# Experts 2 to 5: their weight loads moved behind the last group but one of the eighth tile

## The chip, the cores and the metric

The kernel runs on one core of one Trainium2 chip. The time is device microseconds of one execution. Before the change three runs took 494.34, 494.59 and 498.18 us, median 494.59. One more execution was profiled: it took 492.98 us, of which the profile covers a span of 491.1 us. All times of single instructions below are counted in that span, from its start.

## What is computed

The program filters a signal along its sequence in the frequency domain, and then sends the 19,968 resulting rows through a mixture of eight experts in which every expert keeps at most 80 rows:

```
X = rfft(x, axis=1);  y = irfft(X * (filt_r + i*filt_i));  x = y.reshape(19968, 256)
probs = softmax(x @ w_gate);  expert_idx = argmax;  gate_w = probs of that expert
for e in range(8):
    tok = rows of expert e, of these the 80 with the largest gate_w
    out[tok] = gate_w[tok] * (relu(x[tok] @ w1[e]) @ w2[e])      # all other rows stay zero
```

x has shape (8, 2496, 256), w1 (8, 256, 1024), w2 (8, 1024, 256), all in fp32. One expert's two matrices are 2 x 1024 KB.

## The kernel before

**Stages.** Up to about 300 us the kernel transforms the eight batches and multiplies their spectra with the filter; the spectra go to memory in `yf`, and the gate's logits give the 80 rows that each expert keeps. At most 128 rows a batch are kept, so from there the kernel works on eight tiles of 128 rows, one a batch. For tile t, `fetch` gathers rows of the inverse transform's table (tiles `gts`, two tiles of rows in a buffer), `spectrum` loads the batch's spectrum (`yb`), `turn_rows` transposes the rows on TensorE (L487) with a ScalarE copy (L491), and `add_rows` multiplies them with the spectrum (L498). Each tile goes in five groups of four, and the list `work` holds the groups' transposes ("t") and products ("m") in the order in which TensorE gets them; `go(n)` emits the next n. At the end of a tile the result is copied to `yr` (L503, for the last tile L505 and L506) and written to `y_sel` in memory from ScalarE's queue (L508).

**The experts.** `Experts.gather` (L1040) fetches an expert's 80 rows from `y_sel` by an indirect DMA of GpSimd. The gathers of experts 0 to 2 are emitted before the eighth tile is finished and read only what tiles 0 to 6 wrote; rows of the eighth tile are added by `turn` from `yr` on the core (L1058, beside L1056). So these three gathers wait for the write of the seventh tile's rows. `turn` transposes the rows (L1053 or L1056) and copies them to `xs` (L1061), `layer1` (L1070) and `layer2` (L1085) are the two matrix products, and the result is scattered to `out` (L1090). The order on TensorE is turn 0, layer1 0, turn 1, layer1 1, turn 2, and then for each e: layer2 e, layer1 e+2, turn e+3.

**Order.** The whole is in a manual schedule: each engine gets its instructions in the order in which the code emits them, and waits only for semaphores. Place in the code therefore does not tie a load on SyncE's queue (SP) to a place on TensorE; it ties it to its neighbours on the same queue, and to whatever used its buffer last.

**Weights.** `load_weights` issues two DMAs of 1024 KB on SP (L217 for w1, L219 for w2). Experts 0 and 1 have buffers of their own, asked for after tile 4. Expert 2's buffer is one of the two of `t1pool`, asked for after tile 5, and in the built program it is the one that held the table rows of tiles 4 and 5. Experts 3, 4 and 5 are emitted inside the expert stage, behind `turn(0)`: expert 3 in the spectrum buffer `yx`, expert 4 in one of `ypool`, expert 5 in the other buffer of `t1pool`, which held the rows of tiles 6 and 7. Experts 6 and 7 take the buffers of 0 and 1 when these are done. SP's queue thus holds, in this order, w0, w1, w2, w3, w4, w5, w6, w7.

```
for e in range(NO):
    ex.gather(e, 128 * (B - 1))
go(len(work))
ex.extra = st["yr"], st["last"]
for e in range(3):
    ex.turn(e)
    if e == 0:
        weights(3, st["yx"], "ys")
        weights(4, ypool, "ys")
        weights(5, t1pool, "t1")
```

Of the kernel before, what the change touches and what calls it, by code (L numbers as in the profile page):

```python
# [13 lines left out]
F32 = mybir.dt.float32  # L14
# [9 lines left out]
B, S, C = 8, 2496, 256  # L24
# [13 lines left out]
NDB, NFC = C // 128, FF // 128  # L38
# [43 lines left out]
def kernel(  # L82
# [100 lines left out]
    ypool = ctx.enter_context(tc.tile_pool(name="spec", bufs=NY))  # L183
# [31 lines left out]
    def load_weights(e, w):  # L215
        w1s[e] = w[:, 0:NDB * FF].rearrange("p (k f) -> p k f", k=NDB)
        nc.sync.dma_start(out=w1s[e], in_=moe_w1[e].rearrange("(k p) f -> p k f", p=128))  # L217
        w2s[e] = w[:, NDB * FF:NDB * FF + NFC * C].rearrange("p (k d) -> p k d", k=NFC)
        nc.sync.dma_start(out=w2s[e], in_=moe_w2[e].rearrange("(k p) d -> p k d", p=128))  # L219

    def gather_gates():
        nc.gpsimd.memset(gate[:], 0.0)
        for e in range(E):
            nc.gpsimd.indirect_dma_start(
                out=gate[:, e:e + 1], out_offset=None, in_=gates_dram[:, :],
                in_offset=bass.IndirectOffsetOnAxis(ap=idxt[:, e:e + 1], axis=0),
                bounds_check=N - 1, oob_is_err=False)
# [5 lines left out]
    with ExitStack() as actx:  # L233
        bctx = ExitStack()

        def pool(name, bufs, space=None, within=actx):
            kw = {} if space is None else {"space": space}
            return within.enter_context(tc.tile_pool(name=name, bufs=bufs, **kw))
# [3 lines left out]
        t1pool = pool("t1", 2)  # L242
# [19 lines left out]
        st = {}  # L262
# [204 lines left out]
        def fetch(t):  # L467
            if t % 2 == 0:
                gts[t // 2] = t1pool.tile([128, 2, NS * 128], F32, name=f"gts_{t}", tag="t1")
            nc.gpsimd.indirect_dma_start(  # L470
                out=gts[t // 2][:, t % 2, :], out_offset=None, in_=rows[:, :],
                in_offset=bass.IndirectOffsetOnAxis(ap=idxb[:, t:t + 1], axis=0),
                bounds_check=S - 1, oob_is_err=False)

        def spectrum(t):
            p = ypool if t % NE < NE - 1 else st["yx"]
            ybs[t] = p.tile([128, NS, C], F32, name=f"yb_{t}", tag="ys")
            nc.sync.dma_start(out=ybs[t], in_=yf[t])

        def weights(e, p, tag):  # L480
            load_weights(e, p.tile([128, 2 * NFC * C], F32, name=f"w_{e}", tag=tag))

        def turn_rows(t, g):
            ps = fps.tile([128, SG, 128], F32, name=f"pw_{t}_{g}", tag="f")
            for i in range(SG):
                s = SG * g + i
                nc.tensor.transpose(ps[:, i, :], gts[t // 2][:, t % 2, 128 * s:128 * s + 128],  # L487
                                    ident[:])
            if g % 2 == 0:
                wts[t, g // 2] = xpool.tile([128, 2, SG, 128], F32, name=f"wt_{t}_{g}", tag="x")  # L490
            nc.scalar.copy(out=wts[t, g // 2][:, g % 2], in_=ps[:])  # L491

        def add_rows(t, g):
            if g == 0:
                pos[t] = yps.tile([128, 2, 512], F32, name=f"po_{t}", tag="y")
            for i in range(SG):
                s = SG * g + i
                nc.tensor.matmul(pos[t][:, 0, 0:C], lhsT=wts[t, g // 2][:, g % 2, i, :],  # L498
                                 rhs=ybs[t][:, s, :], start=(s == 0), stop=(s == NS - 1))
            if g == NS // SG - 1:  # L500
                yr = t2pool.tile([128, 2, C], F32, name=f"yr_{t}", tag="t2")
                if t < B - 1:
                    nc.scalar.copy(out=yr[:, 0, :], in_=pos[t][:, 0, 0:C])  # L503
                else:
                    nc.scalar.copy(out=yr[:, 0, 0:128], in_=pos[t][:, 0, 0:128])  # L505
                    nc.vector.tensor_copy(out=yr[:, 0, 128:C], in_=pos[t][:, 0, 128:C])  # L506
                st["yr"] = yr[:, 0, :]
                nc.scalar.dma_start(out=y_sel[128 * t:128 * t + 128, :], in_=yr[:, 0, :])  # L508
# [223 lines left out]
        with tc.manual_schedule():  # L732
# [113 lines left out]
            work = []  # L846
# [8 lines left out]
            def go(n):  # L855
                for kind, t, g in work[:n]:
                    if kind == "t":
                        turn_rows(t, g)
                        if g == NS // SG - 1 and t == NE:
                            fetch(6)  # L860
                            fetch(7)
                    else:
                        add_rows(t, g)
                        if g < NS // SG - 1:
                            continue
                        if t + 3 < B:
                            spectrum(t + 3)
                        if t == NE:
                            gather_gates()
                        if t == 4:  # L870
                            weights(0, wpool, "w")
                            weights(1, wpool, "w")
                        if t == 5:
                            weights(2, t1pool, "t1")
                del work[:n]

            go(1)
            logits(B - 1, 0)
            go(1)
            logits(B - 1, 1)  # L880
            for part in range(4):
                gating(NP - 1, part)
            go(4)
            gating(NP - 1, 4)
            gating(NP - 1, 5)
# [37 lines left out]
                         y_sel[0:128 * B, :], out, idxg, idxs, gate, w1s, w2s)  # L923
            for e in range(NO):
                ex.gather(e, 128 * (B - 1))
            go(len(work))
            ex.extra = st["yr"], st["last"]

            for e in range(3):
                ex.turn(e)  # L930
                if e == 0:
                    weights(3, st["yx"], "ys")
                    weights(4, ypool, "ys")
                    weights(5, t1pool, "t1")
                if e < 2:
                    ex.layer1(e)
            for e in range(E):
# [556 lines left out]
```

## Time and profile before

| what | value |
|---|---|
| median of three runs | 494.59 us |
| the profiled execution's own time | 492.98 us |
| its span | 491.1 us |
| TensorE busy, of the span | 451.3 us (92%) |
| mean of all DMA traffic | 230 GB/s, 112.79 MB |
| end of the eighth tile's last product | 404.3 us |
| layer1 of expert 0 starts | 410.27 us |
| layer1 of expert 2 starts | 432.84 us |

In the timeline each line gives start, duration, engine, source line, operation, tiles out<-in, the number of instructions merged, and in brackets the idle time of that engine before it and what ended it. "SPq" is the issue of a DMA on SyncE's queue, and its duration is that of the issue, not of the transfer. In the table of windows each row is a stretch of time with, for each engine, busy time and (x) the number of instructions, then the granted TensorE clock (1.00 is full speed), the mean busy share of the 16 DMA engines and GB/s.

### The profile page before, as it was taken

What the parts mean: (1) busy time and instruction counts of PE and PEld (TensorE: products, weight loads), DVE (VectorE), ACT (ScalarE), POOL (GpSimd) and SP (SyncE); (2) the same over time, 40 slices, a digit from 0 to 9 for tenths busy, and PEclk for the clock granted to TensorE, in tenths of its full rate; (3) what the DMA queues carried; (4) which work ended last, traced back from release to release, by engine and by line L of the source; (5) the groups of instructions that cost most, each with busy time, mean ns of one, the idle gap of its engine ahead of it and who ended that gap; (6) DMA issues with size and microseconds to landing.
All of it is one profiled execution on the core that took longest, in us unless ns stands there. A gap on an engine that the chain in (4) does not pass through costs nothing. (4 is left out here: it accounts for less than half of the span.)

```text
span 491.1 us, 8653 instructions
## 1 busy us (share of the span) xinstructions
PE 451.3 (92%) x3382; PEld 423.1 (86%) x3382; DVE 202.7 (41%) x582; ACT 221.7 (45%) x339; POOL 176.4 (36%) x244
## 2 busy tenths in 40 slices
PE   5889999999999999999998989977999997999990
PEld 5879999999999999999998978756888877988870
DVE  2154544547845558645488984784000000101100
ACT  3866667666776667676664424310323320011110
POOL 7587344443444435444334471112061020012210
PEclk9999999999999999999999979976999995599996
DMA  7998467778778887889622239929889999065000
GB/s 216 269 276 253 148 211 246 239 252 269 249 240 251 258 262 256 255 256 372 265 85 87 91 111 331 423 76 379 331 316 375 380 381 344 0 192 194 20 17 10
DMA packets 38323, 112.79 MB, mean 230 GB/s; under 512 B 4393, under 2 KB 13923, under 8 KB 36482
## 3 DMA queue, kind: packets, MB, share of 16 engines
q1 hardware_dynamic: 27536, 75.36, 47.1%
q10 hardware_dynamic: 7330, 22.09, 11.5%
q0 software_dynamic: 3408, 14.70, 8.7%
q8 instruction: 29, 0.48, 0.4%
q14 instruction: 20, 0.16, 0.1%
HBM read 68.97 MB, written 43.20 MB: 228 GB/s over the span
## 5 line engine op out<-in xcount | busy, mean ns | idle before, releaser
L346 POOL TENSOR_TENSOR p<-p,p 128x256 f32<-128x256 f32 x160 | 114.5, 736 | 139.0 <-DVE p L340 94.0
L340 DVE TENSOR_TENSOR p<-pb,ft 128x512 f32<-128x512 f32 x160 | 102.2, 680 | 9.6 <-PE pb L332 9.5
L313 ACT COPY t<-pa 128x480 f32<-128x480 f32 x88 | 87.1, 1001 | 26.1 <-PE pa L307 26.1
L307 PE MATMUL pa<-wf_t,x 117*128 117x120 f32 x704 | 93.3, 280 | 6.1 <-DMA x<-in_x_dram 6.0
L307 PEld LDWEIGHTS pa<-wf_t,x 117*128 117x128 f32 x704 | 87.3, 197 | 6.4 <-DMA x<-in_x_dram 5.6
L355 PE MATMUL py<-gi,p 128*128 128x136 f32 x640 | 89.3, 283 | 1.6 <-POOL p L346 1.6
L332 PE MATMUL pb<-d_t,t 128*128 128x128 f32 x640 | 86.0, 278 | 0.0
L355 PEld LDWEIGHTS py<-gi,p 128*128 128x128 f32 x640 | 81.1, 193 | 2.0 <-POOL p L346 2.0
L332 PEld LDWEIGHTS pb<-d_t,t 128*128 128x128 f32 x640 | 78.9, 193 | 0.3 <-issue 0.2
L323 ACT COPY t<-pt 128x512 f32<-128x512 f32 x80 | 46.9, 586 | 68.2 <-PE pt L321 68.2
L498 PE MATMUL po<-yb,wt 128*128 128x256 f32 x240 | 59.3, 393 | 0.6 <-ACT wt L491 0.6
L371 DVE COPY z<-py 128x16 f32<-128x16 f32 x80 | 14.8, 185 | 100.1 <-ACT ysp L367 66.0
L498 PEld LDWEIGHTS po<-yb,wt 128*128 128x128 f32 x240 | 45.3, 199 | 6.2 <-ACT wt L491 0.8
L491 ACT COPY wt<-pw 128x512 f32<-128x512 f32 x40 | 23.3, 586 | 57.4 <-PE pw L487 56.9
L321 PE MATMUL pt<-ident,t 128*128 128x128 f32 x320 | 48.5, 275 | 0.3 <-DVE p L340 0.3
L367 ACT COPY ysp<-py 128x512 f32<-128x512 f32 x60 | 35.3, 589 | 9.9 <-PE py L355 9.9
L321 PEld LDWEIGHTS pt<-ident,t 128*128 128x128 f32 x320 | 38.0, 143 | 0.5 <-DVE p L340 0.5
L1070 PEld LDWEIGHTS ph<-xs,w 128*128 128x128 f32 x256 | 36.2, 227 | 1.8 <-DVE xs L1061 1.3
L1070 PE MATMUL ph<-xs,w 128*128 128x80 f32 x256 | 36.4, 311 | 0.8 <-DVE xs L1061 0.8
L1085 PE MATMUL po<-w,hT 128*80 128x256 f32 x128 | 30.3, 393 | 0.0
L1090 POOL DMA_INDIRECT out_dram<-ys,idxs x8 | 7.5, 935 | 56.3 <-ACT ys L1088 56.3
L487 PEld LDWEIGHTS pw<-ident,gts 128*128 128x128 f32 x160 | 20.4, 145 | 8.0 <-issue 3.7
(176 smaller groups left out, 331.0 us busy)
## 6 DMA issues: line engine op xcount, KB each, us to landing
out_dram<-zero_t SPq DMA_DIRECT2D x64, 312.0 KB
x<-in_x_dram SPq DMA_DIRECT2D x40, 468.0 KB
w<-in_moe_w_dram SPq DMA_DIRECT2D x16, 1024.0 KB
yf<-ysp ACTq DMA_DIRECT2D x30, 512.0 KB
yb<-yf SPq DMA_DIRECT2D x6, 2560.0 KB
yf<-ys ACTq DMA_DIRECT2D x10, 512.0 KB
x<-in_x_dram SPq DMA_DIRECT2D x8, 234.0 KB
d_t<-d_tbl SPq DMA_DIRECT2D x5, 256.0 KB
```

The source lines that it names most:

```text
L307: nc.tensor.matmul(out=ps[:, i, :, 2 * NS * cb:2 * NS * cb + 2 * NS], lhsT=xt[0:NJ * N1, (2 * k + i) % JC, 128 * cb:128 * cb + 128], rhs=w ...
L313: nc.scalar.copy(out=t1[:, 2 * k - h:2 * k - h + 2], in_=ps[:])
L321: nc.tensor.transpose(ps[:, i, cb, :], t1[:, a:a + 2, :].rearrange("p r n -> p (r n)"), ident[:])
L323: nc.scalar.copy(out=t2[:].rearrange("p i c -> p (i c)"), in_=ps[:].rearrange("p i c q -> p (i c q)"))
L332: nc.tensor.matmul(out=ps[:, cb, i], rhs=d_t[:, 2 * u + i, :], start=True, stop=True, lhsT=t2[:, i, 128 * cb:128 * cb + 128])
L340: nc.vector.tensor_tensor(out=pt, in0=ps[:].rearrange("p c s r q -> p (c s) r q"), in1=f.unsqueeze(2).to_broadcast([128, 2 * NDB, 2, NQ]), ...
L346: nc.gpsimd.tensor_tensor(out=yt[:, :, r, :], in0=yt[:, :, r, :], in1=pr[1][:, :, 1 - r, :], op=op)
L355: nc.tensor.matmul(out=ps[:, i, ZW * cb:ZW * cb + ZW], rhs=gi[:, cb, :], lhsT=yt[:, 2 * cb + i].rearrange("p r q -> p (r q)"), start=True, ...
L367: nc.scalar.copy(out=dst, in_=ps[:, :, E:E + C])
L498: nc.tensor.matmul(pos[t][:, 0, 0:C], lhsT=wts[t, g // 2][:, g % 2, i, :], rhs=ybs[t][:, s, :], start=(s == 0), stop=(s == NS - 1))
L1070: nc.tensor.matmul(ph[:, fc // 4, fc % 4, 0:cap], lhsT=self.w1s[e][:, k, 128 * fc:128 * fc + 128], rhs=xs[:, k, :], start=(k == 0), stop=( ...
L1085: nc.tensor.matmul(po[0:cap, :], lhsT=hT[:, fc, :], rhs=self.w2s[e][:, fc, :], start=(fc == 0), stop=(fc == NFC - 1))
```

## The change

The load of expert 2 behind tile 5 is taken out, and so are the loads of experts 3, 4 and 5 behind `turn(0)`. In their place all four are emitted together, between the last group but one and the last group of `work`, before the eighth tile's last products. The tiles are asked for first, in the order 4, 2, 3, 5, and the loads follow in the order 2, 3, 4, 5. The code asks `t1pool` for expert 4's tile and then for expert 2's, `yx` for expert 3's and `ypool` for expert 5's.

```diff
+        def room(e, p, tag):
+            return p.tile([128, 2 * NFC * C], F32, name=f"w_{e}", tag=tag)
+
         def weights(e, p, tag):
-            load_weights(e, p.tile([128, 2 * NFC * C], F32, name=f"w_{e}", tag=tag))
+            load_weights(e, room(e, p, tag))
...
                             weights(1, wpool, "w")
-                        if t == 5:
-                            weights(2, t1pool, "t1")
...
-            go(len(work))
+            go(len(work) - 1)
+            rooms = {4: room(4, t1pool, "t1"), 2: room(2, t1pool, "t1"),
+                     3: room(3, st["yx"], "ys"), 5: room(5, ypool, "ys")}
+            for e in range(2, 6):
+                load_weights(e, rooms[e])
+            go(1)
             ex.extra = st["yr"], st["last"]

             for e in range(3):
                 ex.turn(e)
-                if e == 0:
-                    weights(3, st["yx"], "ys")
-                    weights(4, ypool, "ys")
-                    weights(5, t1pool, "t1")
                 if e < 2:
                     ex.layer1(e)
```

## The prediction

> **What bounds the kernel now.** I read the page first: TensorE (PE) is busy 92% of the span, and its clock row shows two slices of fives near the end. The chain of work that ended last is short here (the last scatter), so I followed PE in the timeline around the change instead, then SP's queue, then the windows.
>
> Timeline of PE, GpSimd and ScalarE from the end of the eighth tile:
>
> ```profile
> 394.31 0.39 ACTq L508 DMA_DIRECT2D y_sel<-yr  x1
> ...
> 401.91 0.94 POOL L1040 DMA_INDIRECT xg<-y_sel,idxg  x1 [26.75 <-ACT wt L491]
> 403.16 0.95 POOL L1040 DMA_INDIRECT xg<-y_sel,idxg  x1 [0.30 <-issue]
> 404.42 0.95 POOL L1040 DMA_INDIRECT xg<-y_sel,idxg  x1 [0.30 <-issue]
> ...
> 407.89 0.69 PE L1056 MATMUL px<-ident,xg 80*128 80x80 f32 x2 [3.62 <-DMA xg<-y_sel,idxg]
> ...
> 410.27 7.12 PE L1070 MATMUL ph<-xs,w 128*128 128x80 f32 x32 [0.42 <-DVE xs L1061]
> ...
> 454.43 3.69 PE L1070 MATMUL ph<-xs,w 128*128 128x80 f32 x32
> ```
>
> The seventh tile's rows are written from 394.31. Only at 401.91 does the first gather go out (the wait list of the built program names this write; the ScalarE copy in the bracket ended earlier), and its rows land at 407.7. PE finished the eighth tile at 404.3 and stands still for 3.62 us. After that the same 32 products of layer1 take 7.12 us for experts 0 and 1 and 3.69 us for the later ones. The windows say why:
>
> ```profile
> 388.00:394.30 6.30, 6.30 (x37) 5.56 (x36) 0.00 (x0) 1.98 (x4) 0.00 (x0) 1.00 1.07 387
> 394.30:400.80 6.50, 6.50 (x38) 5.74 (x37) 0.00 (x0) 1.76 (x3) 0.00 (x0) 1.00 1.06 383
> 400.80:403.50 2.70, 2.70 (x15) 2.37 (x14) 0.00 (x0) 0.59 (x1) 1.28 (x2) 1.00 1.08 366
> 403.50:408.00 4.50, 0.88 (x5) 0.48 (x3) 0.29 (x1) 0.27 (x1) 1.56 (x2) 0.91 1.05 377
> 408.00:417.00 9.00, 8.58 (x40) 8.37 (x40) 0.33 (x1) 0.00 (x0) 0.95 (x1) 0.50 0.99 348
> 417.00:428.00 11.00, 10.58 (x50) 10.37 (x50) 1.31 (x3) 0.88 (x2) 0.00 (x0) 0.50 0.01 3
> 428.00:433.00 5.00, 5.00 (x18) 3.29 (x18) 0.32 (x1) 0.00 (x0) 0.00 (x0) 0.69 0.00 0
> 433.00:440.00 7.00, 7.00 (x51) 5.98 (x51) 0.72 (x2) 0.91 (x2) 1.95 (x2) 1.00 0.82 277
> ```
>
> The clock falls to 0.50 within the gap and stays there until about 431. The DMA engines are full (share 0.99 and more) from 388 to 417 and empty from there to 433. So the stage is bound by a gather that is slow amid weight traffic, and by the clock that the gap costs. What that traffic is, SP's queue shows:
>
> ```profile
> 382.99 4.12 SPq L217 DMA_DIRECT2D w<-in_moe_w_dram  x1
> 387.16 0.46 SPq L219 DMA_DIRECT2D w<-in_moe_w_dram  x1
> 387.74 5.80 SPq L217 DMA_DIRECT2D w<-in_moe_w_dram  x1
> 393.59 0.65 SPq L219 DMA_DIRECT2D w<-in_moe_w_dram  x1
> 394.32 4.77 SPq L217 DMA_DIRECT2D w<-in_moe_w_dram  x1
> 399.14 0.83 SPq L219 DMA_DIRECT2D w<-in_moe_w_dram  x1
> 400.84 3.54 SPq L217 DMA_DIRECT2D w<-in_moe_w_dram  x1
> 404.43 1.40 SPq L219 DMA_DIRECT2D w<-in_moe_w_dram  x1
> ```
>
> These pairs are experts 2, 3, 4 and 5. None waits for `turn(0)` (407.89), behind which three of them stand in the code: SP runs ahead. Expert 5's starts when PE has turned the eighth tile's last rows (400.8), which lay in its buffer.
>
> **The change part by part.**
>
> *Place on SP.* Eight DMA issues move in the code; past each other and past nothing else on SP: its order is still w0 to w7. On PE, ScalarE, VectorE and GpSimd the built program has the same instructions in the same order, so nothing is added there: 0 us.
>
> *Buffers.* Here the code and the built program part. Read as a rotation, expert 2 would get the buffer of the last tiles' rows and could not start before 400.8, with 3, 4 and 5 queued behind it. In the built program it does not: the load of w2 has the same wait list as before (the gathers of tiles 4 and 5, and PE's count at their last transposes), and it is w4 that has the list w5 had (the gathers of tiles 6 and 7, PE's count at 400.8). The pool hands out its two buffers in the order in which the loads write them, not that in which the tiles are asked for. So w2 and w3 go out at 383 and 387.7 as now. w4 is held from 394.32 to 400.84, 6.5 us, and behind it on SP stand w5, w6 and w7.
>
> *Who waits for w4 and w5.* Weights are moved at about 383 GB/s, 2.1 MB an expert, 5.5 us and some share for the rest. The traffic of w0 to w5 ends at 416.5 (9.0 us at 348 GB/s and then 3 GB/s), so with six times 5.8 us w0 began at 382, w3 ends near 405 and w4 follows. By bytes, too: 8.4 MB (w0 to w3) are asked for by 394.2, some 4.7 MB moved, 3.7 MB or 9 us to go, until 403 to 405. An issue into an empty queue starts moving within 2 us (w6: issued 433.25, 211 GB/s already in 434 to 436, none in 432 to 434), so w4's bytes are there by about 402.8, and w5 is asked for 4 us behind it as now. DMA traffic has no hole, or one of at most 1 us near 404. layer1 of expert 4 starts at 447, of expert 5 at 454; their weights land by about 411 and 417. The cover is over 30 us: 0 us. w6 and w7 wait for buffers freed at 433 and 440: 0 us.
>
> *The gap itself.* The write at 394.31 and the gathers at 401.91 to 405.4 meet, up to 404, bytes of w2 and w3 that are asked for as before, and then w4. For the gather the trace has both ends: 5.8 us from issue to landing in full traffic (this one), 2.3 us in a quiet queue (the scatter at 448.6). The write took 7.6 us until the gather went out; the same 2.3 us bounds it below, and the slowest row in traffic is 14.8 us for a gather of gate values near 365, which bounds either above. With traffic unchanged I take the same rows again, and give 0.3 us for a hole near 404: -0.3 us.
>
> *Sum.* Against the profiled execution 492.98 - 0.3 = 492.7. It lies 1.6 us under the median 494.59, so a median of about 494.3.
>
> [...] The clock is what makes the gap dear: full again only after 23 us, while PE was busy. By bounds from rows, closing the gap saves from 404.3 to layer1 of expert 2 (now 28.5 us): turn 0 with its copy 1.4, layer1 3.69, turn 1 with copy 1.4, layer1 3.69, turn 2 1.0, layer2 3.4, 14.6 in all, so 14 us. [...]
>
> **Rivals.**
> 1. *It does as its words say, or the gap closes anyway.* If no weights moved between w1's end (about 393.5) and 402, the write would land near 397, the gathers near 400 to 402, before PE wants them at 404.3: 494.6 - 14 = 480.6. For it: the code's order of asking, and that with w4 held the queue is less deep when the gather goes out. Against: the built program's waits, and w2 and w3 fill the engines until 403 to 405 either way. Halfway cases (rows 1 to 2 us earlier, clock still lost) give 492.6 to 493.6, inside "same". It decides once the first gather's rows land before about 405.
> 2. *The bunch hits the gathers.* w4 and w5 are issued back to back at 400.84 into a queue that isn't full, just when three gathers go out. If the first gather then took the 9.9 us of the median gate gather instead of 5.8, the gap grows by 4.1: 498.7; at 14.8 us, by 9.0: 503.6. Against: now, too, w4's tail and w5 are issued at the same moment, and the engines can't be more than full. It decides from a gather of 10.7 us (over 1%).
> 3. *Expert 4 waits for its weights.* This needs w4 to land 36 us later than reckoned. Nothing in the trace speaks for it; below 1 in 100.
>
> **How the numbers follow.** Unchanged traffic, gap and half clock as before: 0.82, at 494.3; the three runs of before and the profiled one scatter from 492.98 to 498.18 by themselves, and half of the chance of halfway cases lies in it. Rival 1: 0.12, at 480.6. Rival 2, with all else that could slow it: 0.06. One per cent, about what a measurement of this kernel tells from no change, is 4.9 us: faster 0.12, same 0.82, slower 0.06. The range from 490.5 to 498.5 leaves out rival 1 and most of rival 2, and little of the main case, under 2 in 10.
>
> **What would show it.** In the profile after: on SP w2 issued near 383, w3 near 388, w4 at 400.8 and w5 at its heels; DMA share near 1.0 from 388 to 417; the first gather near 401.9; PE idle over 3 us before L1056; clock 0.50 until about 431; layer1 of experts 0 and 1 at 7.1 us. I am wrong if w2 goes out only at 400.8, if the DMA share falls between 394 and 400, or if layer1 of expert 0 takes 3.7 us.

## The result and the profile after

The kernel after takes 495.75 us (median of 20 runs, 491.63 to 497.82), the kernel before beside it 495.83 us (20 runs, 492.81 to 499.43): a ratio of 0.9998, 95% interval 0.9974 to 1.0021. No difference can be measured. The profiled execution of after took 494.47 us (span 492.7). In the text after the diff, the lines of the code stand lower by two or three: the write of the rows is L511, the gather L1042, the transposes of the gathered rows L1058, layer1 L1072.

SP's own queue in the timeline of after (start, time of the issue, in us), the four pairs from expert 2 to expert 5:

```profile
384.88 3.88 SPq L217 DMA_DIRECT2D w<-in_moe_w_dram  x1
388.81 0.46 SPq L219 DMA_DIRECT2D w<-in_moe_w_dram  x1
389.38 5.83 SPq L217 DMA_DIRECT2D w<-in_moe_w_dram  x1
395.27 0.64 SPq L219 DMA_DIRECT2D w<-in_moe_w_dram  x1
402.10 0.37 SPq L217 DMA_DIRECT2D w<-in_moe_w_dram  x1
402.52 0.46 SPq L219 DMA_DIRECT2D w<-in_moe_w_dram  x1
403.03 3.00 SPq L217 DMA_DIRECT2D w<-in_moe_w_dram  x1
406.08 1.89 SPq L219 DMA_DIRECT2D w<-in_moe_w_dram  x1
```

Experts 2 and 3 are asked for early, as before, and it is the third pair, expert 4's, that waits (from 395.9 to 402.1) for the turned rows to leave their buffer. This execution runs some 1.3 us behind that of before by then.

The timeline of after, ScalarE's write, GpSimd's first gather and PE:

```profile
395.57 0.33 ACTq L511 DMA_DIRECT2D y_sel<-yr  x1
...
403.58 0.94 POOL L1042 DMA_INDIRECT xg<-y_sel,idxg  x1 [26.80 <-ACT wt L494]
...
409.92 0.69 PE L1058 MATMUL px<-ident,xg 80*128 80x80 f32 x2 [4.39 <-DMA xg<-y_sel,idxg]
...
412.30 7.12 PE L1072 MATMUL ph<-xs,w 128*128 128x80 f32 x32 [0.42 <-DVE xs L1063]
...
434.68 3.69 PE L1072 MATMUL ph<-xs,w 128*128 128x80 f32 x32
```

The write still takes 8.0 us until the gather can go out (7.6 before), PE still stands idle (4.39 us, 3.62 before), and layer1 of expert 0 still runs at half speed. The windows of after (start and end, PE busy in us, weight loads, VectorE, ScalarE, GpSimd, granted clock, DMA share, GB/s):

```profile
394.30:400.80 6.50, 6.50 (x37) 5.73 (x36) 0.00 (x0) 2.13 (x4) 0.00 (x0) 1.00 1.05 379
400.80:403.50 2.70, 2.70 (x16) 2.37 (x15) 0.00 (x0) 0.59 (x1) 0.00 (x0) 1.00 1.05 389
403.50:408.00 4.50, 2.02 (x10) 1.44 (x8) 0.29 (x1) 0.27 (x1) 2.83 (x3) 1.00 1.07 383
408.00:417.00 9.00, 6.67 (x30) 6.48 (x31) 0.32 (x1) 0.00 (x0) 0.94 (x1) 0.52 1.06 364
417.00:428.00 11.00, 10.58 (x50) 10.37 (x50) 0.82 (x2) 0.44 (x1) 0.00 (x0) 0.50 0.06 23
428.00:433.00 5.00, 5.00 (x21) 3.95 (x21) 0.82 (x2) 0.44 (x1) 0.00 (x0) 0.57 0.00 0
```

The DMA engines are full up to 417 without the hole that holding four experts would have made, and the clock is at 0.50 until after 428. Where the write's 8 us go can be read in the DMA view, by queue (packets, MB, share): q1 carries the weights, q10 the write. First from 395.5 to 399.5, then from 399.5 to 402.5:

```profile
q1 hardware_dynamic: 1084, 1.46, 105.8%
```

```profile
q1 hardware_dynamic: 461, 1.07, 91.4%
q10 hardware_dynamic: 144, 0.13, 12.8%
```

For nearly 4 us after its issue (395.57) no packet of the write moves; all 144 move between 399.5 and 402.5, 143 of them by 402.0, and the gather goes out at 403.58.

### The profile page after: what moved, and what is told of

Read it like the earlier page. It is cut to its first block, busy times and chain, and to the rows that moved or that the text cites. A ratio compares the mean times of both kernels' runs of the same rounds, so it can differ in the third digit from the quotient of the medians.

```text
span 492.7 us, 8652 instructions
## 1 busy us (share of the span) xinstructions
PE 449.9 (91%) x3382; PEld 423.1 (86%) x3382; DVE 203.0 (41%) x582; ACT 221.0 (45%) x339; POOL 176.6 (36%) x244
## 5 line engine op out<-in xcount | busy, mean ns | idle before, releaser
L332 PE MATMUL pb<-d_t,t 128*128 128x128 f32 x640 | 87.1, 280 | 2.1 <-remote 2.1
L332 PEld LDWEIGHTS pb<-d_t,t 128*128 128x128 f32 x640 | 79.9, 195 | 2.5 <-remote 2.2
L501 PE MATMUL po<-yb,wt 128*128 128x256 f32 x240 | 57.6, 385 | 0.6 <-ACT wt L494 0.6
L501 PEld LDWEIGHTS po<-yb,wt 128*128 128x128 f32 x240 | 44.2, 194 | 5.8 <-ACT wt L494 0.8
L1072 PEld LDWEIGHTS ph<-xs,w 128*128 128x128 f32 x256 | 36.2, 227 | 1.8 <-DVE xs L1063 1.3
L1072 PE MATMUL ph<-xs,w 128*128 128x80 f32 x256 | 36.4, 311 | 0.8 <-DVE xs L1063 0.8
L1078 DVE TENSOR_SCALAR hT<-ph 128x320 f32<-128x320 f32 x8 | 3.9, 492 | 55.6 <-ACT hT L1077 49.2
```

The source lines that it names most:

```text
L332: nc.tensor.matmul(out=ps[:, cb, i], rhs=d_t[:, 2 * u + i, :], start=True, stop=True, lhsT=t2[:, i, 128 * cb:128 * cb + 128])
L1072: nc.tensor.matmul(ph[:, fc // 4, fc % 4, 0:cap], lhsT=self.w1s[e][:, k, 128 * fc:128 * fc + 128], rhs=xs[:, k, :], start=(k == 0), stop=( ...
```

## The experiments

The theory to be tested: the change is without effect because it holds only expert 4; the loads of experts 2 and 3 keep the DMA engines full while the rows are written and gathered; the late rows make a gap on PE; the gap costs the clock; and most of the 14 us at stake is the clock, not the wait. Its rivals: the write and the gather are slow of themselves, whatever else moves; the stage's own products (turns and layer1) can't hold the full clock, so that closing the gap brings the wait alone; and the clock would be lost anyway when the stage begins.

One distance tells the cases apart: from the end of the eighth tile's products (the start of what PE does next less its idle time) to layer1 of expert 2, in us of each kernel's own profiled execution. (The profiles come from more than one chip; whole times are compared with runs of before on the same chip.)

| kernel | tile ends | first row transposed | layer1 of expert 2 | distance |
|---|---|---|---|---|
| before | 404.27 | 407.89 | 433.05 | 28.8 |
| after | 405.53 | 409.92 | 434.68 | 29.2 |
| all four held | 407.08 | 407.08 | 422.02 | 14.9 |
| three held (clock lost in this execution) | 408.54 | 409.62 | 433.78 | 25.2 |
| gap filled | 406.38 | 410.61 | 425.16 | 18.8 |
| same products behind the gap | 402.74 | 406.07 | 425.19 | 22.5 |
| three held, gap filled | 406.70 | 409.20 | 423.75 | 17.1 |
| all held, turns filled | 402.57 | 402.57 | 417.93 | 15.4 |

**All four held.** The words of the change made true by hand: expert 2's weights are laid into the buffer of the last tiles' rows itself, not into a tile that the pool hands out.

```diff
-            rooms = {4: room(4, t1pool, "t1"), 2: room(2, t1pool, "t1"),
-                     3: room(3, st["yx"], "ys"), 5: room(5, ypool, "ys")}
-            for e in range(2, 6):
+            w = gts[3][:].rearrange("p i c -> p (i c)")
+            w1s[2] = w[:, 3072:5120].rearrange("p (k f) -> p k f", k=NDB)
+            w2s[2] = w[:, 1024:3072].rearrange("p (k d) -> p k d", k=NFC)
+            nc.sync.dma_start(out=w1s[2], in_=moe_w1[2].rearrange("(k p) f -> p k f", p=128))
+            nc.sync.dma_start(out=w2s[2], in_=moe_w2[2].rearrange("(k p) d -> p k d", p=128))
+            rooms = {3: room(3, st["yx"], "ys"), 4: room(4, t1pool, "t1"),
+                     5: room(5, ypool, "ys")}
+            for e in range(3, 6):
                 load_weights(e, rooms[e])
```

> Expert 2's weights are laid by hand into the tile that held the rows of tiles 6 and 7, so that they wait for its last transposes and experts 3, 4 and 5 queue behind them: the change as its words read. Theory (the traffic of experts 2 and 3 slows the seventh tile's write and the gathers, and the gap costs the clock): no weights move between about 394 and 402, the first gather goes out near 397 instead of 402 to 404, its rows are there before 404, TensorE's gap before turn 0 falls from 3.6 to 4.4 us to under 1, the clock stays at 1.00, layer1 of experts 0 and 1 takes 3.7 us each, and the time falls by about 14 us to 481 to 482 (ratio 0.971). Rival A (the gather is late through GpSimd's or the write's own latency, not the traffic): the gather still goes out after 401 and the time stays within 1%. Rival B (layer1's products of 80 columns can't hold the full clock after a stretch of long products, gap or not): the gap closes and the clock still falls to 0.50, time lower by about 4 us (ratio 0.992).

Measured: 480.9 us (478.76 to 483.24, 4 runs) against 495.3 for before on the same chip, ratio 0.9692, interval 0.9623 to 0.976. The timeline of this kernel, SP's first held issue among it:

```profile
397.29 0.33 ACTq L511 DMA_DIRECT2D y_sel<-yr  x1
...
399.91 0.94 POOL L1047 DMA_INDIRECT xg<-y_sel,idxg  x1 [21.71 <-DMA y_sel<-yr]
...
403.81 0.37 SPq L931 DMA_DIRECT2D gts<-in_moe_w_dram  x1
...
407.08 0.35 PE L1063 MATMUL px<-ident,xg 80*128 80x80 f32 x2
...
408.91 3.80 PE L1077 MATMUL ph<-xs,w 128*128 128x80 f32 x32 [0.42 <-DVE xs L1068]
...
422.02 3.69 PE L1077 MATMUL ph<-xs,gts 128*128 128x80 f32 x32
```

Its windows:

```profile
394.30:400.80 6.50, 6.50 (x37) 5.73 (x36) 0.00 (x0) 2.13 (x4) 0.89 (x1) 1.00 0.22 73
400.80:403.50 2.70, 2.70 (x17) 2.37 (x16) 0.00 (x0) 0.59 (x1) 1.94 (x3) 1.00 0.20 53
408.00:417.00 9.00, 8.14 (x71) 7.84 (x71) 1.04 (x3) 0.44 (x1) 0.87 (x1) 1.00 1.06 375
```

And the DMA view from 397.2 to 398.8, by queue:

```profile
q10 hardware_dynamic: 144, 0.13, 24.2%
```

With none of experts 2 to 5 asked for before 403.81, the write's 144 packets are through by 398.8 (142 of them move between 398.0 and 398.6), the gather follows the write by 2.6 us instead of 8.0, and the transposes begin with no idle time in front of them. The clock stays at 1.00, and layer1 of experts 0 and 1 takes 3.80 us. The rivals "slow of themselves" and "the stage can't hold the clock" fall. Expert 2's weights, asked for 19 us later than in after (403.81 for 384.88), are waited for by nobody; none of PE's waits between 400 and 470 is for a weight, and layer1 of expert 2 begins 14.9 us behind the tile's end, where the bound from rows was 14.6.

**Three held.** Expert 2 is asked for behind tile 5, as in before; only 3, 4 and 5 stand behind the last group but one.

```diff
+                        if t == 5:
+                            weights(2, t1pool, "t1")
...
-            rooms = {4: room(4, t1pool, "t1"), 2: room(2, t1pool, "t1"),
-                     3: room(3, st["yx"], "ys"), 5: room(5, ypool, "ys")}
-            for e in range(2, 6):
+            rooms = {3: room(3, t1pool, "t1"), 4: room(4, st["yx"], "ys"),
+                     5: room(5, ypool, "ys")}
+            for e in range(3, 6):
```

> Expert 2's weights as before (asked for near 383), expert 3's in the buffer of the last tiles' rows, so that experts 3, 4 and 5 wait until 401: half the dose. Theory: traffic ends near 398 and begins again near 402.5. The write issued at 394.3 meets traffic for 4 of its 7.6 us and should land 1 to 2 us earlier, the first gather goes out near 400 and lands near 403 to 406; the gap shrinks to 0 to 2 us, and the time lands between no change and 14 us less: by about 3 us if the clock is still lost, by 12 to 14 if it is not. Rival A (own latency): no change of the gather's start, ratio 1.00.

Measured: 482.66 us over all six executions, but they fall into two groups: 480.41, 481.73, 482.39 and 482.93; and 489.85 and 493.44. The ratio to before, 0.9713 (0.9654 to 0.9772), leaves the last two out. The profiled execution is the slowest, and its timeline and one window show what it lost:

```profile
398.59 0.33 ACTq L511 DMA_DIRECT2D y_sel<-yr  x1
...
404.66 0.94 POOL L1044 DMA_INDIRECT xg<-y_sel,idxg  x1 [26.30 <-DMA w<-in_moe_w_dram]
...
409.62 0.42 PE L1060 MATMUL px<-ident,xg 80*128 80x80 f32 x2 [1.08 <-DMA xg<-y_sel,idxg]
...
411.13 6.36 PE L1074 MATMUL ph<-xs,w 128*128 128x80 f32 x32 [0.42 <-DVE xs L1065]
```

```profile
408.00:417.00 9.00, 7.50 (x42) 6.98 (x41) 0.62 (x2) 0.27 (x1) 0.10 (x1) 0.72 1.05 366
```

What is left of one expert's load in front (0.84 MB between 398.6 and 401.0, when the write's first packets move) is enough to make the write take 6.1 us. The rows then come 1.08 us too late, and in this execution the clock falls to 0.50 near 412.0 (mean 0.72 from 408 to 417): 25.2 us of distance instead of 14.9. That the short gap is the cause is argued, not shown; for it speaks that "all four held", with the same work on PE and no gap, keeps the clock. That the 489.85 lost it in the same place is likely by its time, but it was not profiled. Nor were the four shorter ones, so how long their gaps were is not known.

How so short a gap can be enough was not shown. PE came to a stand at 408.54, and the whole gap, the short transposes and the first 0.9 us of layer1 lie between that and the clock's fall, 3.5 us later.

**Gap filled.** The kernel before, with eight products of 256 columns behind the eighth tile, where PE would stand idle. They compute something that nobody reads, and so do the products added in the next three experiments; nothing else of the kernel is changed. The trace has two records for each of these fp32 products: eight are x16, and what the prediction calls 32 products of layer1 are 16.

```diff
             go(len(work))
+            for i in range(8):
+                nc.tensor.matmul(pos[B - 1][:, 1, 0:C], lhsT=wts[B - 1, 2][:, 0, i % SG, :],
+                                 rhs=ybs[B - 1][:, i, :], start=True, stop=True)
```

> The kernel before with eight more products of 256 columns (3.6 to 3.8 us at full clock) behind the eighth tile's last one, written to a half of the same PSUM tile that nobody reads. The gather is as late as before, only TensorE isn't idle meanwhile. Theory (the idle gap takes the clock away, and layer1 alone can't bring it back): turn 0 starts at about 408 as before, the clock stays at 1.00, layer1 of experts 0 and 1 takes 3.7 us, and the time falls by about 10 us to 485 (ratio 0.98). Rival B (the clock falls through layer1's small products themselves): clock 0.50 from about 411 on, ratio 1.00. Rival C (the clock falls through the DMA traffic or what else happens at that time): the same as B.

Measured: 486.07 us (484.9 to 487.75, 4 runs), ratio 0.9812, interval 0.9751 to 0.9873. Timeline and one window:

```profile
396.42 0.33 ACTq L508 DMA_DIRECT2D y_sel<-yr  x1
...
403.71 0.95 POOL L1043 DMA_INDIRECT xg<-y_sel,idxg  x1 [27.45 <-ACT wt L491]
...
407.06 3.72 PE L928 MATMUL po<-yb,wt 128*128 128x256 f32 x16 [0.68 <-DVE yr L506]
410.61 0.35 PE L1059 MATMUL px<-ident,xg 80*128 80x80 f32 x2
...
412.05 3.80 PE L1073 MATMUL ph<-xs,w 128*128 128x80 f32 x32 [0.42 <-DVE xs L1064]
```

```profile
408.00:417.00 9.00, 8.32 (x61) 7.68 (x59) 0.92 (x3) 0.44 (x1) 0.94 (x1) 1.00 1.06 377
```

The write is as slow as ever (7.3 us), DMA as full, the first row is transposed 4.2 us behind the tile's end: only PE's standing still is gone, and with it the half clock. The distance falls from 28.8 to 18.8. So of the 13.9 us between before and "all four held", 10.0 are the clock's in these executions. The other 3.9 are the wait's at most, since the eight products end only just before the first row is transposed and may hold it up themselves. By the medians the two parts are 9.2 and 5.2 us, and the intervals leave each some 3 us either way.

**The same products behind the gap.** The same eight products stand behind the turn of expert 0's rows.

```diff
                 ex.turn(e)
                 if e == 0:
+                    for i in range(8):
+                        nc.tensor.matmul(pos[B - 1][:, 1, 0:C], lhsT=wts[B - 1, 2][:, 0, i % SG, :],
+                                         rhs=ybs[B - 1][:, i, :], start=True, stop=True)
                     weights(3, st["yx"], "ys")
```

> The kernel before with the same eight products of 256 columns, but behind turn 0, after the gap instead of in it (unread, as in e3). The gap stays, the clock falls in it. Theory (once the clock is at half, the sparse stream of layer1 can't raise it and a dense stream can): the products run at half clock at first, 0.9 us each, the clock is back at 1.00 after 4 to 7 us of them, about 415, both layer1 take 3.7 to 4.5 us, and layer1 of expert 2 starts at 429 to 430 instead of 433 to 434.7 although 3.7 us of work at full clock were added: ratio 0.988 to 0.997. Rival (the clock comes back a fixed time, some 24 us, after it fell, whatever runs): the products cost 7.2 us at half clock, clock 0.50 until about 431, ratio 1.01.

Measured: 485.19 us (485.03 to 487.92, 4 runs) against 490.44 (488.54 to 494.31, 11 runs) for before on this chip, ratio 0.99, interval 0.9851 to 0.9948. Timeline and windows:

```profile
406.07 0.42 PE L1059 MATMUL px<-ident,xg 80*128 80x80 f32 x2 [3.33 <-DMA xg<-y_sel,idxg]
...
407.00 5.34 PE L933 MATMUL po<-yb,wt 128*128 128x256 f32 x16
```

```profile
402.70:406.80 4.10, 0.77 (x8) 0.76 (x7) 0.29 (x1) 0.27 (x1) 0.77 (x1) 1.00 1.05 369
406.90:410.20 3.30, 3.30 (x11) 2.68 (x10) 0.33 (x1) 0.00 (x0) 0.26 (x1) 0.52 1.07 394
410.30:414.00 3.70, 3.70 (x26) 3.42 (x26) 0.00 (x0) 0.00 (x0) 0.58 (x1) 0.98 1.06 380
```

This was to show whether the eight products help by keeping the clock or in another way. The gap is there (3.33 us), the clock does fall, and after some 3.4 us of these products it is back. So the clock doesn't need some 24 us to come back, whatever runs. The products cost 5.34 us on the path and still bring 1%: in before and after, the clock had not come back in 17.8 us of layer1 and turns (0.50 from 410.27 to 428.1 and from 412.3 to 430.1). There it came back at 431.10 and 432.31, under layer2's products of 256 columns, which begin at 428.12 and 430.16.

**Three held, gap filled.** The second experiment with four such products behind the last group.

```diff
             go(1)
+            for i in range(4):
+                nc.tensor.matmul(pos[B - 1][:, 1, 0:C], lhsT=wts[B - 1, 2][:, 0, i % SG, :],
+                                 rhs=ybs[B - 1][:, i, :], start=True, stop=True)
```

> e2 (experts 3 to 5 held) with four such products, 1.8 us, behind the eighth tile's last one, where e2 has a gap of about 1 us. Theory (e2 lost the clock in its slow executions only because a gap of 1 us and the sparse work around it can still take it away): no execution loses the clock; all lie at 481 to 484, none at 490 or more; ratio 0.972 to 0.976. Rival (those executions were disturbed by something else): again one in three near 490.

Measured: 480.31 us (478.77 to 483.42, 5 runs), ratio 0.9774, interval 0.9735 to 0.9813. A ratio of 0.972 to 0.976 was expected. The five lie within 1%. The unfilled kernel's two long executions would lie at 485.0 and 488.6 on this chip, if they scale as before does (490.44 to 495.3), and none of the five does. The profiled execution, the longest of them:

```profile
407.38 1.99 PE L936 MATMUL po<-yb,wt 128*128 128x256 f32 x8 [0.68 <-DVE yr L509]
409.20 0.35 PE L1063 MATMUL px<-ident,xg 80*128 80x80 f32 x2
...
410.64 3.80 PE L1077 MATMUL ph<-xs,w 128*128 128x80 f32 x32 [0.42 <-DVE xs L1068]
```

Five executions against a loss in two of six don't prove that it can't happen; they agree with the theory. The clock of this one stays at 1.00 from 394.3 to 428.

**All held, turns filled.** The first experiment with two such products behind the turns of experts 0 and 1, where it still had idle stretches of 0.4 us.

```diff
+                    for i in range(2):
+                        nc.tensor.matmul(pos[B - 1][:, 1, 0:C], lhsT=wts[B - 1, 2][:, 0, i % SG, :],
+                                         rhs=ybs[B - 1][:, i, :], start=True, stop=True)
```

> e1 (experts 2 to 5 held) with two such products, 0.9 us, behind turn 0 and two behind turn 1, where TensorE waits 0.8 us for the copy of the turned rows. They fill waits, so they should cost 0.1 to 0.2 us each time and guard the clock. Theory: time as e1 or up to 0.5 us over it, 480 to 482, ratio 0.969 to 0.973, clock 1.00 until the end.

Measured: 478.6 us (475.5 to 479.8, 6 runs), ratio 0.9743, interval 0.9703 to 0.9783. The interval overlaps that of "all four held" (0.9692), which ran on another chip: nothing is gained that can be told from it, and the distance is 0.5 us longer (15.4), where 0.2 to 0.4 us were expected. The clock could be held without the products. "All four held" is thus the version to keep: 3.1% under before with no extra work.

## Why the prediction was right

*The number.* The forecast of 494.3 us lies 1.45 us under the measured 495.75. Of these, 1.24 us lie in the start of the sum: the three runs of before had a median of 494.59, the 20 runs beside after 495.83.

*Place on SP, and buffers.* Right: expert 2's load and expert 3's went out at 384.9 and 389.4 (near 383 and 388 were said, and the execution is 1.3 us late), expert 4's at 402.1 when the turned rows had left, expert 5's at its heels. The order in which the tiles are asked for doesn't decide; the order of the loads does.

*Who waits for experts 4 and 5.* Right: nobody. "All four held" shows how wide the cover is: there the loads of experts 2 to 5 are issued 4 us (expert 4) to 19 us (expert 2) later than in after, and PE isn't late for one of them.

*The traffic.* Right: full from 388 to 417, with no hole near 404, for which 0.3 us had been given; the write took 8.0 us against 7.6 and the gap was 4.39 against 3.62. Those 0.8 us of one execution are below what the 20 runs can tell. What was not seen beforehand is how the write is late: for nearly 4 us it doesn't begin to move, and then its packets take some 2.5 us, where "all four held" needs 0.6. The slowest row in traffic, given as 14.8 us, is 14.9, a gather of table rows; no term hangs on it.

*The gap and the clock.* Right in the size of the stake: 14 us were reckoned for a closed gap, and 13.9 is the difference of the distances, 14.4 that of the medians (495.3 and 480.9). (The 28.5 us that the prediction starts from end at the weight load of expert 2's layer1, 432.84; its first product starts at 433.05, which gives 28.8.) The first rival's price was sound, then, and only its condition, four experts held, wasn't met by this program. Its point of decision, rows landing before about 405, was not tested closely. In the profiled execution of "three held" they came 1.08 us behind the tile's end, which in before would be 405.35, and the clock was lost.

*The clock's return.* That the clock was full again only after 23 us, with PE busy, goes with layer1's products only. With the eight 256-column products it was back after some 3.4 us: 0.52 from 406.9 to 410.2, 0.98 from 410.3. With layer1's 80-column products, which the records of before and after show as 10.58 us busy of 11.00, it was not: 0.50 from 417 to 428. So being busy in the records did not by itself bring the clock back. The two kinds of products differ in their time per column: at full clock layer1's 16 products of 80 columns take 3.69 us, 2.9 ns a column, and layer2's 8 of 256 take 3.62 us, 1.8 ns a column. Whether that is what counts was not measured.

*The second rival* (the bunch of experts 4 and 5 hits the gathers): not seen. From the first gather's issue to the first transpose it is 6.3 us after (403.58 to 409.92) and 6.0 before.

## What to carry to other kernels

Look in the built program for the waits of each load before you believe a change of buffers: the words of this one were worth 3%, its program nothing. A small write that the path waits for should not be issued behind megabytes of prefetch that nobody needs yet (8.0 us until its reader went out in after, 2.6 in "all four held"); hold the prefetch by a real dependence on what the path does. And price a short gap in front of narrow products by the clock that it can lose, not by its length: here 10.0 of the 13.9 us were the clock's, for a gap of 3.62.

## What the runs showed of the hardware beyond that

A write of 128 KB took 2.6 us until its reader went out with the DMA engines almost empty (share near 0.2), 6.1 us behind what was left of one expert's load, and 8.0 us in full traffic, with no packet moved in nearly the first 4 us.

The four profiled executions that lost the clock behind the eighth tile had it at 0.50 from 407.21 to 431.10 (before), 408.42 to 432.31 (after) and, as worked out from the windows' means, from about 412.0 to 432.5 ("three held") and 407.0 to 410.4 (the products behind the gap). That is 23.9, 23.9, 20.5 and 3.4 us. The loss came 2.9 to 4.3 us after the eighth tile's end, in the last two only after the gap itself was over. Under layer1's 80-column products and the turns it lasted through 17.8 us (before and after), and one stretch of 3.4 us of 256-column products ended it. What a gap of about 1 us costs was seen in one profiled execution only (1.08 us, "three held").

The kernel before itself took 495.3 us on one chip and 490.44 on another, so whole times were compared within one chip only.
